# The up-projections of a bilinear MLP by Strassen's seven products over pairs of token blocks

## The chip, the cores and the metric

One core of one Trainium2 chip. The metric is the time of one execution on the device in microseconds (us); lower is better. The profile is one execution of the kernel before; a page and a trace of it are quoted below.

## What is computed

Chunked attention over 64-token chunks gives x (2304 tokens, 512 columns). A first MLP with PReLU and a second, bilinear MLP follow, all in fp32:

```python
def _moe_ref(x, w_in, w_out, alpha):
    h = x @ w_in                                  # 512 -> 2048
    g = np.maximum(h, 0.0) + alpha * np.minimum(h, 0.0)
    return g @ w_out                              # 2048 -> 512

def _moe2_ref(x, w_a, w_b, w_out):
    a = x @ w_a                                   # 512 -> 1536
    b = x @ w_b
    return a * b @ w_out                          # 1536 -> 512
```

The weights arrive as 64-bit floats; the kernel turns them into 32-bit ones itself.

## The kernel before

**Blocks.** The 2304 tokens are five blocks, four of 512 and one of 256 (the second). TensorE (PE) works on float32r operands: every fp32 operand is split into a high part (ScalarE, ACT: `to_hi`, L79) and a low part (VectorE, DVE: `to_lo`, L82), and each product is three matmuls, hi·hi, hi·lo and lo·hi (`three`, L366).

**MLP1.** For each block, J1 = 16 slices j of 128 hidden columns: `s1` (4 x 3 matmuls into a `psh` bank), `prelu` (two ACT, one DVE, then the split into gh, gl), and `s2` (4 x 3 matmuls into four `acc` banks), which runs two slices late (`flush(2)`). In blocks 0 to 3 the attention of the next block is done between these steps. At a block's end `end1` copies the four banks to DRAM (`x2d`), but for the last block, whose result is split directly into the operand of MLP2.

**MLP2.** Blocks outermost (`order2`: the last block first, the short one last), J2 = 12 slices inside. `s3` makes b and a (each 4 x 3 matmuls), multiplies them and splits the product c into ch, cl; `s4` (four token groups, 3 matmuls each, two groups in the short block) adds c times w_out into the `acc` banks, one slice late (`flush(1)`). So PE always has the next `s3` while ACT and DVE make c.

```python
pb = proj(W["b", j], x, n)[:, :n]
...
pa = proj(W["a", j], x, n)[:, :n]
nc.vector.tensor_tensor(out=b_sb, in0=pa, in1=b_sb, op=ALU.mult)
...
split(ch, cl, b_sb)
```

**Weights.** `units` lists 128-column slices in the order of need. `w_load` brings one (512 KB) into one of three staging buffers through SP's queue; `unpack_ops` makes fp32 of it (one ACT at L124, three DVE at L128, L133, L136); `split(*w_parts(i))` makes its two parts. All 36 slices of MLP2 stay in SBUF once split, and are used by all five blocks.

**What orders the work.** The program is written in the order in which each engine runs it (a manual schedule): every engine and SP's DMA queue take their instructions in that order, and one that waits holds all behind it on the same engine. PSUM has eight banks: four in the pool `acc`, four in the pool `ps`. Other pools that matter: `gp` and `tp` (three buffers each), `sp` (three staging buffers), `xp` (two pairs of 512 x 4 operands), `wp` (72 tiles of 128x512).

## Time and profile before

| what | value |
|---|---|
| median of 3 runs | 897.4 us (897.17 to 897.72) |
| the profiled execution: its span, first to last instruction | 895.8 us |
| PE busy, share of the span | 884.1 us, 99% |
| DVE busy | 402.7 us, 45% |
| ACT busy | 352.6 us, 39% |
| mean granted TensorE clock | 0.996 of full |
| DMA: bytes moved | 79.48 MB, mean 89 GB/s |

The profile states a span for its execution and no other time; the median of the runs lies 1.6 us above it. Busy time of PE counts overlapping matmuls once; the pitch of matmuls (from one start to the next) is read from the timeline. A releaser, behind an arrow, is the instruction that ended a wait.

### The profile page before, as it was taken

The page shows a single profiled execution, that of the slowest core. Times are in us where ns is not written, and L with a number is a line of the kernel's source. Part 1 is how long each engine was busy: PE and PEld are TensorE (multiplying, and loading weights), DVE is VectorE, ACT ScalarE, POOL GpSimd, SP SyncE. Part 2 cuts the span into 40 slices and gives each one's busy share as a digit, 9 for nine tenths or more (in the row PEclk, how much of TensorE's full clock was granted, in tenths as well). Part 3 has the DMA queues.
Part 4 walks back from the last instruction along what each step waited for, and adds up shares of the span by engine and source line. Part 5 has one row for each costly group of instructions (what it writes and reads, how often), then busy time and mean ns, then how long its engine had stood idle before and what let it go on. Part 6 is the DMA issues. An engine that isn't in the chain of part 4 may idle for free.

```text
span 895.8 us, 12893 instructions
## 1 busy us (share of the span) xinstructions
PE 884.1 (99%) x5298; PEld 743.9 (83%) x5298; DVE 402.7 (45%) x762; ACT 352.6 (39%) x636; POOL 0.7 (0%) x6
## 2 busy tenths in 40 slices
PE   7999999999999999999999999999999999999998
PEld 6878889988888888888888888888888888888897
DVE  5999955454434443388756742111211122111221
ACT  5687765555436343466534422111211122111211
POOL 0000000000000000000000000000000000000000
PEclk9899999999999999999999999999999999999999
DMA  9686767455425320444414312000020002000100
GB/s 213 199 263 196 213 165 178 107 155 129 106 60 146 79 56 5 141 142 141 148 64 136 124 46 93 2 1 0 1 95 1 0 1 71 1 1 0 48 1 23
DMA packets 127498, 79.48 MB, mean 89 GB/s; under 512 B 94160, under 2 KB 116176, under 8 KB 127440
## 3 DMA queue, kind: packets, MB, share of 16 engines
q1 hardware_dynamic: 127152, 78.41, 31.0%
q8 instruction: 41, 0.67, 0.3%
q10 hardware_dynamic: 288, 0.26, 0.1%
q14 instruction: 17, 0.14, 0.1%
HBM read 53.49 MB, written 16.78 MB: 78 GB/s over the span
## 4 chain that ended last, share of the span: by engine, by line
PE 92%; DVE 6%; ACT 2%; issue 1%; ACTq 0%; POOLq 0%; DVEq 0%; POOL 0%
PE psh L366 52%; PE acc L366 37%; DVE wx L136 1%; PE psSO L291 1%; PE psSO L342 1%; DVE wz L128 1%; DVE wz L133 1%; DVE gl L82 0%; PE psT L278 0%; DVE sm L317 0%; PE warm L625 0%; PE psP L330 0%; DVE e L321 0%; DVE mx L304 0%; DVE e L306 0%
## 5 line engine op out<-in xcount | busy, mean ns | idle before, releaser
L442 DVE TENSOR_TENSOR b_sb<-psh,b_sb 128x512 f32<-128x512 f32 (+1 forms) x60 | 38.3, 638 | 273.2 <-PE psh L366 273.2
L386 DVE SCALAR_TENSOR_TENSOR pos<-neg,nalpha_sb,pos 128x512 f32<-128x512 f32 (+1 forms) x80 | 55.6, 695 | 107.3 <-ACT pos L385 107.0
L440 ACT ACTIVATE b_sb<-psh 128x512 f32<-128x512 f32 (+1 forms) x60 | 33.1, 552 | 168.2 <-PE psh L366 168.2
L79 ACT ACTIVATE ch<-b_sb 128x512 fp32r<-128x512 f32 (+1 forms) x60 | 35.3, 589 | 153.6 <-DVE b_sb L442 153.6
L82 DVE TENSOR_TENSOR gl<-pos,gh 128x512 fp32r<-128x512 f32 (+1 forms) x80 | 51.1, 638 | 43.5 <-ACT gh L79 43.5
L79 ACT ACTIVATE gh<-pos 128x512 fp32r<-128x512 f32 (+1 forms) x80 | 47.2, 590 | 59.0 <-DVE pos L386 59.0
L384 ACT ACTIVATE neg<-psh 128x512 f32<-128x512 f32 (+1 forms) x80 | 43.8, 548 | 40.4 <-PE psh L366 40.4
L82 DVE TENSOR_TENSOR cl<-b_sb,ch 128x512 fp32r<-128x512 f32 (+1 forms) x60 | 38.3, 639 | 39.3 <-ACT ch L79 39.3
L136 DVE SCALAR_TENSOR_TENSOR wx<-wx,wz 128x512 int32<-128x512 int32 x68 | 46.8, 689 | 4.7 <-ACT wx L124 0.8
L124 ACT ACTIVATE wx<-raw 128x512 f32<-128x512 f32 x68 | 42.7, 669 | 4.0 <-DMA raw<-in_moe_w_b_dram 3.8
L385 ACT ACTIVATE pos<-psh 128x512 f32<-128x512 f32 (+1 forms) x80 | 44.2, 553 | 0.0
L128 DVE TENSOR_SCALAR wz<-raw 128x512 uint16<-128x512 uint16 x68 | 29.8, 462 | 3.2 <-DMA raw<-in_moe_w_b_dram 3.2
L133 DVE TENSOR_SCALAR wz<-raw 128x512 uint16<-128x512 uint16 x68 | 31.0, 455 | 0.0
L242 ACT ACTIVATE kqd<-kq 128x1024 uint16<-128x1024 uint16 x24 | 23.9, 1047 | 0.3 <-DMA kq<-in_k_dram 0.3
L79 ACT ACTIVATE xh<-psSO 128x256 fp32r<-128x256 f32 x28 | 8.9, 384 | 25.0 <-PE psSO L342 25.0
L312 ACT ACTIVATE e<-e 128x512 f32<-128x512 f32 x18 | 11.3, 629 | 13.6 <-DVE e L306 13.4
L242 ACT ACTIVATE ed<-e 128x1024 uint16<-128x1024 uint16 x8 | 8.5, 1058 | 17.2 <-DVE e L321 13.6
L321 DVE TENSOR_TENSOR e<-e,rc 128x512 f32<-128x512 f32 x18 | 12.4, 691 | 0.6
L317 DVE TENSOR_REDUCE sm<-e 128x8 f32<-128x512 f32 x18 | 12.2, 680 | 1.0 <-ACT e L312 0.8
L82 DVE TENSOR_TENSOR xl<-psSO,xh 128x256 fp32r<-128x256 f32 x28 | 10.2, 415 | 1.5 <-ACT xh L79 1.5
L304 DVE TENSOR_REDUCE mx<-psSO 128x4 f32<-128x256 f32 x28 | 10.5, 418 | 0.7 <-ACT xh L79 0.7
L291 PEld LDWEIGHTS psSO<-kT,qT 64*64 64x64 f32 x448 | 7.7, 134 | 3.7 <-issue 2.8
(731 smaller groups left out, 2505.7 us busy)
## 6 DMA issues: line engine op xcount, KB each, us to landing
raw<-in_moe_w_out_dram SPq DMA_DIRECT2D x28, 512.0 KB, 3.5
raw<-in_moe_w_in_dram SPq DMA_DIRECT2D x16, 512.0 KB, 4.6
raw<-in_moe_w_b_dram SPq DMA_DIRECT2D x12, 512.0 KB, 4.7
raw<-in_moe_w_a_dram SPq DMA_DIRECT2D x12, 512.0 KB, 3.8
v<-in_v_dram SPq DMA_DIRECT2D x16, 256.0 KB, 4.2
out_dram<-os SPq DMA_DIRECT2D x8, 512.0 KB, 2.8
rowsk<-kqd SPq DMA_DIRECT2D x12, 256.0 KB, 2.1
rowsq<-kqd SPq DMA_DIRECT2D x12, 256.0 KB, 2.5
```

What stands on the lines that cost most here:

```text
L79: nc.scalar.activation(out=hi, in_=src, func=AF.Copy)
L82: nc.vector.tensor_tensor(out=lo, in0=src, in1=hi.bitcast(F32), op=ALU.subtract)
L124: return nc.scalar.activation(out=x.bitcast(F32), in_=hw.bitcast(F32), func=AF.Copy, scale=2.0 ** -112)
L128: yield nc.vector.tensor_scalar(out=z2[:, :, 0], in0=h2[:, :, 1], scalar1=13, scalar2=None, op0=ALU.logical_shift_right)
L133: yield nc.vector.tensor_scalar(out=z2[:, :, 1], in0=h2[:, :, 3], scalar1=1 << 15, scalar2=None, op0=ALU.bitwise_and)
L136: yield nc.vector.scalar_tensor_tensor(out=x, in0=x, scalar=3, in1=z, op0=ALU.logical_shift_left, op1=ALU.bitwise_or)
L366: nc.tensor.matmul(out=ps, lhsT=a, rhs=b, start=(i == 0 and first), stop=(i == n_i - 1 and a is wl))
L384: nc.scalar.activation(out=neg, in_=h, func=AF.Relu, scale=-1.0)
L385: yield nc.scalar.activation(out=pos, in_=h, func=AF.Relu)
L386: yield nc.vector.scalar_tensor_tensor(out=pos, in0=neg, scalar=nalpha_sb[:, j:j + 1], in1=pos, op0=ALU.mult, op1=ALU.add)
L440: nc.scalar.activation(out=b_sb, in_=pb, func=AF.Copy)
L442: nc.vector.tensor_tensor(out=b_sb, in0=pa, in1=b_sb, op=ALU.mult)
```

## The change

MLP2 is put in another order, and its up-projections are computed in another way.

- **Pairs.** The blocks of 512 tokens form two pairs, (0, 2) and (3, 4). With the pair's two blocks as rows, the two halves of the 512 inputs, and w_a, w_b as a 2 x 2 arrangement of halves, seven products of half depth (2 x 3 matmuls each) stand where there were eight. `pair_group(p, j)` issues them into three PSUM banks (A, B, D), three of them added onto a bank that already holds a product, and combines them with seven DVE operations and two ACT copies. The short block keeps its two full products (`rest_group`).
- **Operands.** `sums` and `summed` make four sums of token halves for each pair and split them; for pair 0 the inputs are read from DRAM during the last MLP1 block, for pair 1 two come from DRAM and two straight from the `acc` banks of MLP1's last block (`late_pair`). `weights_steps(j)` unpacks w_a, w_b of slice j, makes four differences (tT) and splits all into T[j] (two buffers).
- **Order.** Slices outermost: for each j the groups of pair 0, the short block (r) and pair 1. Small steps wait in a list `todo2`; `background(us)` takes steps worth so many us out of it at fixed places of a group; `need` takes all up to a mark.
- **c and w_out.** c goes to DRAM unsplit (`keep`); the unpacked w_out is stored to DRAM (`pd`) during the last MLP1 block and read back after pair 0's last group. The last product is a stage of its own at the end: each c is loaded, split, and multiplied, two loads ahead.

```diff
+    full = [b for b in range(NBLK) if sizes[b] == NB]
+    odd = [b for b in range(NBLK) if sizes[b] < NB]
+    pairs = list(zip(full[0::2], full[1::2]))
...
+    order2 = full + odd
+    Q = KD * P // 2
...
-    units += [(m, j) for j in range(J2) for m in "bap"]
+    units += [("p", j) for j in range(J2)] + [(m, j) for j in range(J2) for m in "ab"]
...
-    def s3(j, x, n):
-        pb = proj(W["b", j], x, n)[:, :n]
...
-        nc.scalar.activation(out=b_sb, in_=pb, func=AF.Copy)
...
-        cl = gp.tile([P, NB], F32R, tag="gl", name="cl")[:, :n]
...
-        return ch, cl
+    cd = {(b, j): dr.tile([P, n], F32, name=f"cd{b}_{j}") for b, n in enumerate(sizes) for j in range(J2)}
+    pd = [dr.tile([P, DM], F32, name=f"pd{j}") for j in range(J2)]
+    def keep(b, j, c):
+        nc.sync.dma_start(out=cd[b, j], in_=c)
...
+    def operand(p, q):
+        X[p, q] = [(wtile(f"x{p}{q}h"), wtile(f"x{p}{q}l")) for _ in range(2)]
...
+        for kk in range(2):
+            nc.sync.dma_start(out=X[p, q][kk][1].bitcast(F32), in_=x2d[b][:, 2 * half + kk])
...
+    def sums(p, kk, a21, a22):
...
+        t = {}
+        SUB = ALU.subtract
+        return t, [
+            (0.69, lambda: tt("s1", a21, a22, ALU.add)),
+            (0.69, lambda: tt("s2", lambda: t["s1"], lambda: src("11"), SUB)),
+            (0.69, lambda: tt("s3", lambda: src("11"), a21, SUB)),
+            (0.69, lambda: tt("s4", lambda: src("12"), lambda: t["s2"], SUB)),
+        ]
+    def summed(p, kk, t):
+        def one(q):
+            hl = X[p, q][kk]
+            return [(0.0, lambda: to_hi(*hl, t[q])), (0.69, lambda: to_lo(*hl, t[q]))]
+        return stagger([one(q) for q in ("s1", "s2", "s3", "s4")])
...
+    def stagger(chains):
+        steps = [c[0] for c in chains[:1]]
+        for i, c in enumerate(chains):
+            steps += [d[0] for d in chains[i + 1:i + 2]] + c[1:]
+        return steps
...
+    def weights_steps(j):
...
+        th, tl = xtiles("T")
+        T[j] = th.rearrange("p k n -> p (k n)"), tl.rearrange("p k n -> p (k n)")
+        ua, ub = (units.index((m, j)) for m in "ab")
...
+        def tt(q, a, b):
+            if "t" not in t:
+                t["t"] = sp.tile([P, 2 * DM], F32, tag="stg", name="tT")
+            nc.vector.tensor_tensor(
+                out=t["t"][:, q * Q:(q + 1) * Q], in0=a(), in1=b(), op=ALU.subtract
+            )
...
+        return [
+            (0.0, lambda: (begin(ua), begin(ub))),
+            (0.46, lambda: go(ua)), (0.46, lambda: go(ua)),
+            (0.69, lambda: end(ua, "a")),
+            (0.46, lambda: go(ub)), (0.46, lambda: go(ub)),
+            (0.0, lambda: hi(ca, "a")),
+            (0.69, lambda: end(ub, "b")),
+            (0.0, lambda: hi(cb, "b")),
+            (0.4, lambda: tt(0, part("b", 0), part("a", 0))),
+            (0.4, lambda: tt(1, part("b", 1), part("t", 0))),
+            (0.4, lambda: tt(2, part("b", 1), part("b", 0))),
+            (0.4, lambda: tt(3, part("a", 1), part("t", 1))),
+            (0.0, lambda: hi(ct, "t")),
+            (0.69, lambda: lo(ca, "a")),
+            (0.69, lambda: lo(cb, "b")),
+            (1.2, lambda: lo(ct, "t")),
+        ]
...
+    def product(ps, p, q, j, w, start):
+        th, tl = T[j]
+        for kk in range(2):
+            f = slice(w * Q + kk * P, w * Q + (kk + 1) * P)
+            (wh, wl), (xh, xl) = (th[:, f], tl[:, f]), X[p, q][kk]
+            for i, (a, b) in enumerate(((wh, xh), (wh, xl), (wl, xh))):
+                nc.tensor.matmul(
+                    out=ps, lhsT=a, rhs=b, start=(start and kk == 0 and i == 0),
+                    stop=(kk == 1 and i == 2), skip_group_check=not start,
+                )
...
+    def background(us):
+        while todo2 and us > 0:
+            cost, fn = todo2.pop(0)
+            us -= cost
+            fn()
...
+    def need(key):
+        while key not in ready:
+            todo2.pop(0)[1]()
...
+    def pair_group(p, j, new_bank):
+        A, B, D = (new_bank(nm) for nm in ("psA", "psB", "psD"))
...
+        product(A, p, "11", j, 0, True)
+        p1 = tmp(gp, "gh", "p1")
+        nc.scalar.activation(out=p1, in_=A, func=AF.Copy)
+        product(B, p, "s2", j, 5, True)
+        t1 = tmp(gp, "gl", "t1")
+        tt(t1, p1, B)
+        product(D, p, "s1", j, 4, True)
+        p5 = tmp(tp, "t", "p5")
+        nc.scalar.activation(out=p5, in_=D, func=AF.Copy)
+        product(A, p, "12", j, 1, False)
+        product(B, p, "s3", j, 6, False)
+        background(2.7)
+        t2 = tmp(tp, "t", "t2")
+        tt(t2, p1, B)
+        tt(p5, t2, p5)
+        product(D, p, "s4", j, 3, False)
+        product(B, p, "22", j, 7, False)
+        tt(t1, t1, D)
+        tt(t1, A, t1, ALU.mult)
+        keep(pairs[p][0], j, t1)
+        tt(p1, p1, B)
+        tt(p1, p1, p5, ALU.mult)
+        keep(pairs[p][1], j, p1)
+        background(1.2)
...
+    def rest_group(j):
+        th, tl = T[j]
+        n = sizes[odd[0]]
...
+        pb = half(slice(DM, 2 * DM))
+        b_sb = tp.tile([P, NB], F32, tag="t", name="b_sb")[:, :n]
+        nc.scalar.activation(out=b_sb, in_=pb, func=AF.Copy)
+        pa = half(slice(0, DM))
+        background(2.0)
+        nc.vector.tensor_tensor(out=b_sb, in0=pa, in1=b_sb, op=ALU.mult)
+        keep(odd[0], j, b_sb)
...
+    BG = [0.0, 0.0] + [2.6] * 12 + [6.0, 6.0]
...
+        def go():
+            next(gen[0])
+        def end():
+            next(gen[0])
+            nc.sync.dma_start(out=pd[j], in_=xs.pop(i).bitcast(F32))
+        return [(0.0, begin), (0.46, go), (0.46, go), (0.69, end)]
...
+        done["p"] = 0
+        for j in range(1, 13):
+            early2.setdefault(j, []).append(p_next)
+        early2[1].insert(0, first)
+        for j, fn in (
+            (3, lambda: sums_at(0)), (4, lambda: sums_out(0)), (5, lambda: sums_at(1)), (6, lambda: sums_out(1)),
+            (8, lambda: directs(0, ("11",))), (9, lambda: directs(0, ("12",))), (10, lambda: directs(0, ("22",))),
+            (11, rest_in),
+            (11, lambda: (w_dma(U_AB + 2), todo2.extend(weights_steps(0)))),
+            (13, lambda: (fetch(1, "11", b3, 0), fetch(1, "12", b3, 1))),
+        ):
+            early2[j].append(fn) if j in early2 else early2.update({j: [fn]})
...
+    def late_pair(acc):
...
+        for kk in range(2):
+            def a22(kk=kk):
+                t["a22", kk] = a = wtile("a22", F32)
+                nc.scalar.activation(out=a, in_=acc[2 + kk], func=AF.Copy)
+            t[kk], four = sums(1, kk, lambda kk=kk: acc[kk], lambda kk=kk: t["a22", kk])
+            steps += [(0.0, a22)] + four
+        for kk in range(2):
+            steps += summed(1, kk, t[kk])
+        for kk in range(2):
+            hi, lo = X[1, "22"][kk]
+            steps += [
+                (0.0, lambda hi=hi, lo=lo, kk=kk: to_hi(hi, lo, t["a22", kk])),
+                (0.69, lambda hi=hi, lo=lo, kk=kk: to_lo(hi, lo, t["a22", kk])),
+            ]
+        for q in ("11", "12"):
+            steps += stagger([settled(1, q, kk) for kk in range(2)])
+        todo2.extend(steps)
...
-                if b == NBLK - 1 and j >= 2:
-                    ready = NU1 + 3 * (j - 2) // 2
-                    w_dma(ready + 3)
-                    w_unpack(ready + 1)
-                    w_split(ready)
+                if b == NBLK - 1:
+                    for step in early2.get(j, ()):
+                        step()
+                    background(BG[j] if j < len(BG) else 9.0)
...
+        background(99.0)
+        w_dma(U_AB + 4)
+        mark((0, 0))
+        todo2.extend(weights_steps(1))
+        mark((0, 1))
+        background(3.0)
         flush(0)
...
+        late_pair(acc[0])
+        mark((1, 0))
+        mark((1, 1))
+        seq = [(0, 0), ("r", 0), (0, 1), (1, 0), ("r", 1), (1, 1)]
+        for j in range(2, J2 - 1):
+            seq += [(0, j), ("r", j), (1, j)]
+        seq += [(0, J2 - 1), (1, J2 - 1), ("r", J2 - 1)]
+        left = {j: 3 for j in range(J2)}
+        built = 1
+        for p, j in seq:
+            if j < 2 and p != "r":
+                need((p, j))
+            if p == "r":
+                rest_group(j)
+            else:
+                pair_group(p, j, bank if p == 0 else acc_bank)
+            left[j] -= 1
+            if not left[j] and built + 1 < J2:
+                background(99.0)
+                built += 1
+                w_dma(U_AB + 2 * built + 4)
+                todo2.extend(weights_steps(built))
+            if (p, j) == (0, J2 - 1):
+                for i in range(J2):
+                    W["p", i] = hl = wtile(f"wp{i}h"), wtile(f"wp{i}l")
+                    nc.sync.dma_start(out=hl[1].bitcast(F32), in_=pd[i])
+                todo2.extend(stagger([settle_w(i) for i in range(J2)]))
+        background(99.0)
...
+        order = [(b, j) for b in order2 for j in range(J2)]
+        cs = {}
...
+        def load_c(i):
+            if i < len(order):
+                b, j = order[i]
+                n = sizes[b]
+                hi = gp.tile([P, NB], F32R, tag="gh", name="ch")[:, :n]
+                lo = gp.tile([P, NB], F32R, tag="gl", name="cl")[:, :n]
+                nc.sync.dma_start(out=lo.bitcast(F32), in_=cd[b, j])
+                cs[i] = hi, lo
...
+        for i in range(2):
+            load_c(i)
+        for i, (b, j) in enumerate(order):
+            c = cs.pop(i)
+            split(*c, c[1].bitcast(F32))
+            load_c(i + 2)
...
+            def second(b=b, j=j, c=c):
+                if j == 0:
+                    acc[0] = new_acc()
+                s4(j, c, acc[0], sizes[b])
+                if j == J2 - 1:
+                    end2(b, acc[0])
+            pend.append(second)
+            flush(1)
```

Three places show how the order of the instructions moved. First DVE, where MLP2 begins to need MLP1's last block. Before, after the last `gl` of MLP1 (xl, xh is the operand, wz, wx an unpacking weight, psh a PSUM bank):

```order
L82 TENSOR_TENSOR gl<-pos,gh 128x512
L128 TENSOR_SCALAR wz<-raw 128x512
L133 TENSOR_SCALAR wz<-raw 128x512
L136 SCALAR_TENSOR_TENSOR wx<-wx,wz 128x512
L82 TENSOR_TENSOR wb6l<-wx,wb6h 128x512
L82 TENSOR_TENSOR xl<-acc,xh 128x512 x4
L442 TENSOR_TENSOR b_sb<-psh,b_sb 128x512
```

In the change, between the last operation of group (0, 1) and the first of group (1, 0), DVE has (ss is a sum, x1..h and x1..l the parts of pair 1's operands; three more rows like those of x1s1l to x1s3l, with the sums of the second half, are left out):

```order
L603 TENSOR_TENSOR p_5171<-p_5171,p_5187 128x512
L488 TENSOR_TENSOR ss_5232<-x112l,ss_5207 128x512
L87 TENSOR_TENSOR x1s1l<-ss_5154,x1s1h 128x512
L87 TENSOR_TENSOR x1s2l<-ss_5156,x1s2h 128x512
L87 TENSOR_TENSOR x1s3l<-ss_5158,x1s3h 128x512
L87 TENSOR_TENSOR x1s4l<-ss_5201,x1s4h 128x512
L87 TENSOR_TENSOR x1s4l<-ss_5232,x1s4h 128x512
L87 TENSOR_TENSOR x122l<-a_5152,x122h 128x512
L87 TENSOR_TENSOR x122l<-a_5203,x122h 128x512
L87 TENSOR_TENSOR x111l<-x111l,x111h 128x512 x2
L87 TENSOR_TENSOR x112l<-x112l,x112h 128x512 x2
L603 TENSOR_TENSOR t_5279<-p_5271,psB 128x512
```

Four splits have become one sum and fourteen splits in a row; the product that opens group (1, 0) reads x111.

Second DVE inside a slice. Before, in the first block of MLP2:

```order
L136 SCALAR_TENSOR_TENSOR wx<-wx,wz 128x512
L82 TENSOR_TENSOR wp10l<-wx,wp10h 128x512
L82 TENSOR_TENSOR wb11l<-wx,wb11h 128x512
L442 TENSOR_TENSOR b_sb<-psh,b_sb 128x512
L82 TENSOR_TENSOR cl<-b_sb,ch 128x512
```

In the change, in group (0, 3), two combining operations that read bank B, and between them the unpacking of the next slice's weights:

```order
L603 TENSOR_TENSOR t_5647<-p_5639,psB 128x512
L129 TENSOR_SCALAR wz<-raw 128x512
L134 TENSOR_SCALAR wz<-raw 128x512
L137 SCALAR_TENSOR_TENSOR wx<-wx,wz 128x512
L129 TENSOR_SCALAR wz<-raw 128x512
L134 TENSOR_SCALAR wz<-raw 128x512
L137 SCALAR_TENSOR_TENSOR wx<-wx,wz 128x512
L603 TENSOR_TENSOR t_5682<-p_5639,psB 128x512
```

Before, the unpacking stood behind the product of a slice; now it stands between two reads of a bank that PE writes again.

Third SP's DMA queue towards the end. Before, it held the reload of the next block and the output (xr is a reloaded block, os and ot staged outputs):

```order
L475 DMA xr<-x2d_90 128x1024 x2
L497 DMA out_dram<-os 128x2x512 x2
L475 DMA xr<-x2d_88 128x2x256 x2
L497 DMA out_dram<-os 128x2x512 x2
L491 DMA out_dram<-ot 128x256 x2
```

In the change, from pair 0's last group to the first loads of c (cd is c in DRAM, pd the unpacked w_out there; wp2l to wp10l, which are alike, are left out):

```order
L442 DMA cd_11_98<-t_7069 128x512
L442 DMA cd_11_122<-p_7061 128x512
L1043 DMA wp0l<-pd_147 128x512
L1043 DMA wp1l<-pd_148 128x512
L1043 DMA wp11l<-pd_158 128x512
L442 DMA cd_11_134<-t_7165 128x512
L442 DMA cd_11_146<-p_7157 128x512
L442 DMA cd_11_110<-b_sb 128x256
L1056 DMA cl<-cd_0_87 128x512
L1056 DMA cl<-cd_1_88 128x512
```

The twelve loads of w_out and the last three stores of c stand ahead of the first load of c.

## Rows read from the trace of the kernel before

**Rows 1.** The page: busy time and share by engine; the chain that ended last.
```profile
PE 884.1 (99%) x5298; PEld 743.9 (83%) x5298; DVE 402.7 (45%) x762; ACT 352.6 (39%) x636; POOL 0.7 (0%) x6
PE 92%; DVE 6%; ACT 2%; issue 1%; ACTq 0%; POOLq 0%; DVEq 0%; POOL 0%
```

**Rows 2.** The chain in order of time from 380 us: start, us, what.
```profile
441.00 8.16 PE acc L366 x36
449.16 10.88 PE psh L366 x48
...
829.96 5.44 PE psh L366 x24
...
886.34 2.87 PE psh L366 x24
```

**Rows 3.** Timeline, PE and ACT around 604 us: start, us, engine, instruction.
```profile
603.81 0.39 PE L366 MATMUL psh<-yh,wb7l 128*128 128x512 f32 x1
604.04 0.39 PE L366 MATMUL psh<-yh,wa7h 128*128 128x512 f32 x1
...
604.30 0.60 ACT L440 ACTIVATE b_sb<-psh 128x512 f32<-128x512 f32 x1 [4.07 <-PE psh L366]
```

**Rows 4.** DVE by form: busy us, mean ns of one | idle before.
```profile
L136 DVE SCALAR_TENSOR_TENSOR wx<-wx,wz 128x512 int32<-128x512 int32 x68 | 46.8, 689 | 4.7 <-ACT wx L124 0.8
L442 DVE TENSOR_TENSOR b_sb<-psh,b_sb 128x512 f32<-128x512 f32 x48 | 33.2, 692 | 238.1 <-PE psh L366 238.1
L133 DVE TENSOR_SCALAR wz<-raw 128x512 uint16<-128x512 uint16 x68 | 31.0, 455 | 0.0
L306 DVE TENSOR_TENSOR e<-psSO,mx 128x256 f32<-128x256 f32 x28 | 10.4, 415 | 0.0
L82 DVE TENSOR_TENSOR yl<-xr,yh 128x1024 fp32r<-128x1024 f32 x6 | 7.3, 1225 | 1.5 <-ACT yh L79 1.5
```

**Rows 5.** Timeline of DVE in MLP1's last block.
```profile
430.38 0.69 DVE L136 SCALAR_TENSOR_TENSOR wx<-wx,wz 128x512 int32<-128x512 int32 x1
430.99 0.68 DVE L82 TENSOR_TENSOR wa4l<-wx,wa4h 128x512 fp32r<-128x512 f32 x1
431.59 0.69 DVE L82 TENSOR_TENSOR wp4l<-wx,wp4h 128x512 fp32r<-128x512 f32 x1
...
438.23 0.69 DVE L82 TENSOR_TENSOR gl<-pos,gh 128x512 fp32r<-128x512 f32 x1 [0.70 <-ACT gh L79]
```

**Rows 6.** ACT by form: busy us, mean ns of one | idle before.
```profile
L124 ACT ACTIVATE wx<-raw 128x512 f32<-128x512 f32 x68 | 42.7, 669 | 4.0 <-DMA raw<-in_moe_w_b_dram 3.8
L79 ACT ACTIVATE ch<-b_sb 128x512 fp32r<-128x512 f32 x48 | 30.3, 632 | 135.2 <-DVE b_sb L442 135.2
```

**Rows 7.** DMA issues: count, KB each, median us from issue to landing.
```profile
raw<-in_moe_w_b_dram SPq DMA_DIRECT2D x12, 512.0 KB, 4.7
raw<-in_moe_w_a_dram SPq DMA_DIRECT2D x12, 512.0 KB, 3.8
out_dram<-os SPq DMA_DIRECT2D x8, 512.0 KB, 2.8
rowsk<-kqd SPq DMA_DIRECT2D x12, 256.0 KB, 2.1
...
xr<-x2d SPq DMA_DIRECT2D x2, 256.0 KB, 4.5
...
out_dram<-ot SPq DMA_DIRECT2D x2, 128.0 KB, 1.8
```

**Rows 8.** Windows of 2 us: busy PE, PEld, DVE, ACT, POOL; granted clock, DMA share, GB/s.
```profile
18.00:20.00 2.00, 0.56 (x4) 0.42 (x4) 1.90 (x6) 1.11 (x2) 0.00 (x0) 1.00 1.11 223
20.00:22.00 2.00, 1.31 (x36) 1.20 (x36) 1.58 (x5) 1.89 (x6) 0.00 (x0) 0.71 0.20 6
22.00:24.00 2.00, 1.73 (x39) 1.21 (x41) 1.61 (x5) 1.58 (x3) 0.00 (x0) 0.50 0.26 70
24.00:26.00 2.00, 2.00 (x44) 1.88 (x37) 2.00 (x7) 1.66 (x5) 0.00 (x0) 0.50 0.48 193
26.00:28.00 2.00, 2.00 (x13) 2.00 (x12) 2.00 (x7) 1.24 (x3) 0.00 (x0) 0.58 0.31 54
...
36.00:38.00 2.00, 1.61 (x7) 1.01 (x6) 2.00 (x4) 1.08 (x2) 0.00 (x0) 1.00 0.80 270
```

More of the change, by code (lines that the diff above doesn't have):

```diff
@@ L472, in reload @@
-    def reload(b):
-        for e in range(0, KD, 2):
-            s = sp.tile([P, 2, DM], F32, tag="stg", name="xr")[:, :, :sizes[b]]
-            nc.sync.dma_start(out=s, in_=x2d[b][:, e:e + 2])
-            yield s
-    def resplit(e, s, x2):
-        n = s.shape[2]
-        split(x2[0][:, e:e + 2, :n], x2[1][:, e:e + 2, :n], s)
+            s = sp.tile([P, 2, DM], F32, tag="stg", name="xs")[:, :, :n]
+            copy2(s, acc, e, n)
+            nc.sync.dma_start(out=x2d[b][:, e:e + 2], in_=s)
@@ new lines, in sums, with src, tt @@
+    def sums(p, kk, a21, a22):
+        def src(q):
+            return X[p, q][kk][1].bitcast(F32)
+        def tt(nm, a, b, op):
+            t[nm] = wtile(f"s{nm}", F32)
+            nc.vector.tensor_tensor(out=t[nm], in0=a(), in1=b(), op=op)
+        t = {}
[6 more added lines that the diff above has]
+        ]
@@ new lines, in late_pair @@
+    def late_pair(acc):
+        for q in ("22", "s1", "s2", "s3", "s4"):
+            operand(1, q)
+        t = {}
+        steps = []
+        for kk in range(2):
[14 more added lines that the diff above has]
+            steps += stagger([settled(1, q, kk) for kk in range(2)])
+        todo2.extend(steps)
```

161 lines of the change are left out of this document (113 added, 48 removed).

## The prediction

> **What bounds the kernel now.** I read the page's busy times first: PE is busy for 99% of the span and makes 92% of the chain that ended last, while DVE and ACT stand at 45% and 39% [rows 1]. Then the chain in order of time: from 441 us to the end it is matmuls without a gap, 36 in 8.16 us, then 48 in 10.88 us, to the short block's 24 in 2.87 us [rows 2]. So a matmul of 512 columns costs 8.16/36 = 0.2267 us from start to start, one of 256 columns 2.87/24 = 0.1196 us, and MLP2 begins at 449.16 us with nothing to gain but matmuls: whatever is taken away counts in full, and every new wait of PE counts in full. The timeline gives the price of a hand-over: wb7l's last matmul is followed by the next 0.23 us later, and ACT's copy of the bank starts 0.26 us after that [rows 3]; I use 0.27 us. DVE to ACT and back cost 0.03 to 0.1 us.
>
> **What is taken away.** A pair and slice had 2 x 24 matmuls and has 7 x 6 = 42. Two pairs, 12 slices: 144 matmuls x 0.2267 = **32.6 us less**. The short block and the last product keep their matmuls. A product of six takes 1.36 us, a pair group 9.52 us, the short block's group 2.87 us.
>
> **What is added, and its cover.** Per slice DVE has 14 combining operations at 0.692, two unpackings (2 x (0.455 + 0.455 + 0.689)), four differences at 0.415, splits of 0.692, 0.692 and 1.225 and a short product of about 0.42: 17.6 us [rows 4] under 2 x 9.52 + 2.87 = 21.9 us of PE. So DVE is not the bound on average, and the cost is in places where PE must wait. Back to back, DVE starts independent operations of this size every 0.605 us [rows 5], dependent ones every 0.72 us.
>
> *End of MLP1.* Unpacking w_out, the sums and the splits of pair 0 lie under PE, about 5.0 us of DVE in each 5.44 us slice. Behind the gl of slice 14, whose equivalent ends at 438.9 us [rows 5], stand b's unpacking, the differences and splits of T[0]: 6.3 us with the pitches above, then slice 15's own 2.1 us. Its gl ends at 447.2 us, and the second matmul of its s2 wants it at 441.0 + 24 x 0.2267 + 0.23 = 446.7 us: **0.6 us** (0 to 4, should the loads of pair 0, five of 512 KB and six of 256 KB at once with the stores, hold DVE up).
>
> *Slice 1's weights.* SP sends them only behind the store of the last unpacked w_out, about 1 us before PE starts group (0, 0); w_b is issued 0.5 us later and takes 4.7 us [rows 7], so it lands 4.2 us after that start. ACT has its widening (0.67) and a split (0.63) [rows 6] ahead of the copy p1 (0.60 [rows 3]), which frees bank A only 6.1 us after the start, and the fourth product wants it at 4.08 us: **2.0 us** (0 to 2.5).
>
> *Pair 1's operands.* DVE ends group (0, 1) 1.7 us after PE does (0.27, then two operations). Then come the last sum and ten splits up to the one that PE's second matmul of (1, 0) reads, x111's first: 12 starts at 0.605 = 7.3 us. PE stands from 0.23 to 9.0 us: **8.8 us** (8 to 11; at 0.69 each it is 9.8). Nothing covers it; in the before kernel s3 did, with the operand's four splits under MLP1's last matmuls.
>
> *Slice 2's weights.* They are issued behind the stores of (1, 0), about 2.2 us after it, land 3.8 and 4.7 us after issue [rows 7], and again stand ahead of p1, now of group (1, 1): 1.7 us. T[2] is then finished in a row: its low part of w_a comes 1.9 us after PE wants it, and 0.4 us go at the bank turns. **4.0 us** (2.5 to 6). From slice 3 on loads are a slice ahead.
>
> *Inside pair 0's groups.* Weights of the next slice stand between t1 and t2. t1 starts at 2.72 + 0.27 = 3.0 us; ACT widens w_a only behind p5 (4.35 + 0.6 + 0.65 = 5.6); then wx, two half steps and wx on DVE bring t2 to 7.75 us and its end to 8.45 us, and the product that writes its bank wants to start at 8.16 us: **0.3 us x 9 slices = 2.7 us** (0 to 6).
>
> *w_out and c through DRAM.* SP's order after group (0, 11) is twelve loads, three stores, then c. With 2.7 us for 256 KB (I take it between the 2.1 us of a 256 KB write and the 3.8 us of a 512 KB read) and 0.7 us for each that follows (512 less 256 KB of writes, 2.8 - 2.1) [rows 7], w_out's fourth lands 7.1 us on; its split stands ahead of t2: 0.9 us. After (1, 11) DVE has five splits (3.0 us) ahead of the short product, whose store goes out at 15.9 us; c is issued at 16.4, lands at 19.1 and is split by ACT at 19.7 us. PE ended at 9.52 + 0.9 + 2.87 = 13.3 us. **7.5 us** in all (6 to 11).
>
> *The last stage.* A load may start when the product three before it has ended: 0.3 + 2.7 + 0.05 + 0.63 + 0.05 + 2.72 = 6.5 us against 3 x 2.72 = 8.16 us: hidden, with up to 4.3 us for a load. For the short block, 0.3 + 2.3 + 0.5 + 1.37 = 4.5 us against 4.1 us, three or four times: **1.7 us** (0.5 to 5; 2.3 us lies near the 1.8 us of a 128 KB write).
>
> *The clock.* The granted clock fell to 0.71 and 0.50, half of full and so 1.2 of 2.4 GHz, after 2 us in which PE was busy for 0.56 us, and stayed there while PE was dense again, to within 26 to 28 us [rows 8]. From 24 to 28 us that lost 2 x 0.5 + 2 x 0.42 = 1.8 us, with 20 to 24 us 3.4 us. The two long waits (8.8 and 6.6 us) should each bring this; I take 2.1 us, near the dense part alone: **4.2 us** (0 to 7). The Trainium skill ("TensorE: Matmul & The Clock Gate", Part 1) says that an idle array goes to half clock and must be busy for a while to get it back; this trace agrees.
>
> **The sum.** Waits: 0.6 + 2.0 + 8.8 + 4.0 + 2.7 + 7.5 + 1.7 + 4.2 = 31.5 us. Against 32.6 us that leaves 1.1 us: a span of 894.7 for 895.8, and 897.4 - 1.1 = **896.3 us** for the median, which lies 1.6 us above the span. The forecast is that Strassen's saving is nearly given back, above all in two waits at the borders of the new stages. A measurement here can tell some 0.2%, 1.8 us, from no change.
>
> **Rivals.**
> *Cover is better.* DVE's 45% leaves room, and if the clock stays up or comes back at once, t2 is in time and slice 1's weights arrive early, 4.2 + 2.7 + 2.0 us fall away: 887.4 us. For it: a wait of 0.39 us in the window from 36 to 38 us left the clock at full [rows 8]. Against: the waits of 8.8 and 6.6 us are much longer. 20%.
> *Late in the middle of pair 0's groups: slower.* PE writes bank B again at 8.16 us, my chain ends at 8.45 us, and each 0.1 us more costs 0.9 us. Five hand-overs between ACT and DVE stand in it; at 0.15 us more each the wait is 1.0 us and the time 896.3 + 9 x 0.7 = 902.6 us. It decides from a wait of 0.7 us (899.9 and more). 15%.
> *Loads of c bound the last stage: slower.* If 256 KB take the 4.5 us of the reload behind two output stores [rows 7], the loop is 8.3 to 8.8 us against 8.16: up to 0.6 x 16 = 9.6 us, and the short block 6 us more: 911.9 us. Against: one load at a time, on an idle queue. 5%.
> *The clock swings in every group: slower.* The short waits of nine slices would each cost a spell of half clock, 9 x 2.1 = 19 us: 915.2 us. Rows speak against it (full clock across a 0.39 us wait [rows 8]). The Trainium skill, on the same page ("A second HAM failure mode"), tells of a kernel that cycles through PSUM banks, idles briefly between groups and swings between the two clocks; by that rule this change would be worse off, and no row here shows it. 5%.
> *The change doesn't remove the matmuls.* PE's program is shorter by exactly 144, so I give this nothing.
>
> **How the numbers follow.** The forecast has 55%; its own range is 891 to 901 us from the bounds above, taken as independent. Below 895.6 us it is faster (22 of the 55), within 1.8 us same (20), above 899.2 slower (13). With the rivals: faster 0.22 + 0.20 = 0.42, same 0.20, slower 0.13 + 0.25 = 0.38. The range 887 to 907 us takes in the forecast, better cover and the late middle, and leaves out the last two rivals and tails, under 0.2.
>
> **What would show it.** 144 matmuls fewer; PE idle for about 9 us before x111's product and 6 to 7 us before the first product of the last stage, each followed by a granted clock near 0.5; a wait near 0.3 us before the seventh product of pair 0's groups; none in the last stage's full blocks. I am wrong if PE's waits outside the two borders exceed 15 us, or if either border is covered.

## The result, and the profile after

| kernel | median | range, runs |
|---|---|---|
| before | 897.5 us | 897.17 to 897.72, 4 |
| changed | 902.63 us | 901.62 to 904.39, 4 |

The ratio is 1.0058, 95% interval 1.0044 to 1.0073: slower by 0.6%, 6.3 us above the forecast and inside its range. A run's time is 1.8 us more than its span, before and after. The profiled execution has 899.8 us; its span is 5.1 us above the forecast one.

The page of the changed kernel, to be held against [rows 1] (the PEclk line is the granted clock in 40 slices, in tenths):

```profile
span 899.8 us, 13238 instructions
PE 864.0 (96%) x5154; PEld 717.5 (80%) x5154; DVE 525.9 (58%) x976; ACT 373.5 (42%) x668; POOL 0.7 (0%) x6
PEclk9999999999999999999997999999999999999999
```

144 matmuls are gone, as said, and PE is busy for 20 us less. What it now waits for is in the waits of PE from 440 us on (total, times, longest); the same view of the kernel before is empty in this stretch:

```profile
PE acc L367 <- ACT ch L84: 7.8, 2, 6.0
PE psA L573 <- ACT x111h L84: 4.6, 1, 4.6
PE psA L573 <- ACT p L607: 3.8, 2, 2.3
PE psA L573 <- DVE x111l L87: 3.6, 1, 3.6
PE psA L573 <- DVE Tl L87: 1.7, 1, 1.7
PE psB L573 <- DVE t L603: 1.4, 1, 1.4
PE acc L367 <- DVE gl L87: 0.2, 1, 0.2
```

Where they stand, and what comes behind them, is in PE's timeline (start, duration, engine, instruction, wait before it):

```profile
449.88 0.39 PE L573 MATMUL psA<-x011h,Th 128*128 128x512 f32 x1
...
455.69 0.50 PE L573 MATMUL psA<-x012h,Th 128*128 128x512 f32 x1 [1.57 <-ACT p L607]
...
478.43 0.80 PE L573 MATMUL psA<-x111h,Th 128*128 128x512 f32 x1 [4.56 <-ACT x111h L84]
482.83 0.79 PE L573 MATMUL psA<-x111l,Th 128*128 128x512 f32 x1 [3.60 <-DVE x111l L87]
...
503.41 0.66 PE L573 MATMUL psA<-x112h,Th 128*128 128x512 f32 x1 [2.28 <-ACT p L607]
...
742.78 0.80 PE L367 MATMUL acc<-wp0h,ch 128*128 128x512 f32 x1 [5.99 <-ACT ch L84]
...
881.65 0.50 PE L367 MATMUL acc<-wp3h,ch 128*128 128x512 f32 x1 [1.84 <-ACT ch L84]
...
885.00 0.63 PE L367 MATMUL acc<-wp4h,ch 128*128 128x512 f32 x1
```

Matmuls that take 0.63 us and more are at half clock. First the window that holds the wait at slice 1, 1.57 us, then one at or behind each long wait (columns as in [rows 8]; the granted clock is the figure behind POOL):

```profile
452.00:456.00 4.00, 2.43 (x11) 1.73 (x10) 3.24 (x7) 2.72 (x5) 0.00 (x0) 1.00 0.36 128
480.00:484.00 4.00, 1.17 (x3) 0.98 (x4) 4.00 (x8) 0.00 (x0) 0.00 (x0) 0.50 0.00 0
504.00:508.00 4.00, 4.00 (x13) 3.14 (x12) 2.66 (x7) 2.05 (x3) 0.00 (x0) 0.62 0.35 119
742.00:746.00 4.00, 3.22 (x8) 2.51 (x9) 2.08 (x3) 1.89 (x3) 0.00 (x0) 0.51 0.24 93
882.00:886.00 4.00, 4.00 (x12) 3.07 (x11) 0.86 (x3) 0.42 (x1) 0.00 (x0) 0.57 0.10 33
```

Four spells at half clock, where the forecast had two; the wait of 1.57 us at 455 us brought none.

**The account.** "Lost" is counted so: from each product's first matmul to the next product's I take the difference of the starts, less the product's matmuls at 0.2267 us (0.1196 with 256 columns). What is left over is lost. (The 0.29 us of pair 0's groups are such a loss, spread over the starts of two matmuls; the view of PE's waits has none of them.) The kernel before loses 0.2 us in its whole MLP2, the changed one 36.3 us, and 0.7 more ahead of it:

| term of the forecast | forecast | measured | of it at half clock |
|---|---|---|---|
| End of MLP1 | 0.6 | 0.7 | |
| Slice 1's weights | 2.0 | 1.9 | |
| Pair 1's operands | 8.8 | 10.8 | 1.9 |
| Slice 2's weights | 4.0 | 6.6 | 1.8 |
| Inside pair 0's groups (nine) | 2.7 | 2.6 | |
| w_out and c through DRAM | 7.5 | 9.4 | 1.6 |
| The last stage | 1.7 | 4.7 | 1.7 |
| The clock (in the rows above) | 4.2 | | 7.0 |
| sum | 31.5 | 36.7 | 7.0 |

The parts come to within 0.3 us of 37.0. Against 32.6 us saved that is 4.4 us, and the span is 4.0 us longer.

The last wait's cause, in the chain in order of time (start, duration, what): the load of c stands on SP behind both output stores of the block before, and takes 4.03 us beside them.

```profile
875.64 0.02 ACT os L456
875.66 0.47 issue
876.13 0.42 ACT ch L84
876.55 0.41 SPq L662
...
877.04 4.03 DMA cl<-cd
...
881.18 0.42 ACT ch L84
```

### The profile page after: what moved, and what is told of

Its sections match the earlier page's. It is cut to its first block, busy times and chain, and to the rows that moved or that the text cites. A ratio compares the mean times of both kernels' runs of the same rounds, so it can differ in the third digit from the quotient of the medians.

```text
span 899.8 us, 13238 instructions
## 1 busy us (share of the span) xinstructions
PE 864.0 (96%) x5154; PEld 717.5 (80%) x5154; DVE 525.9 (58%) x976; ACT 373.5 (42%) x668; POOL 0.7 (0%) x6
## 5 line engine op out<-in xcount | busy, mean ns | idle before, releaser
L87 DVE TENSOR_TENSOR cl<-cl,ch 128x512 fp32r<-128x512 f32 (+1 forms) x60 | 38.3, 639 | 109.1 <-ACT ch L84 103.8
L84 ACT ACTIVATE ch<-cl 128x512 fp32r<-128x512 f32 (+1 forms) x60 | 35.3, 589 | 109.4 <-DMA cl<-cd 73.2
L603 DVE TENSOR_TENSOR t<-p,psB 128x512 f32<-128x512 f32 x48 | 32.8, 684 | 56.7 <-PE psB L573 55.1
L607 ACT ACTIVATE p<-psA 128x512 f32<-128x512 f32 x24 | 14.3, 596 | 76.0 <-PE psA L573 75.3
L613 ACT ACTIVATE p<-psD 128x512 f32<-128x512 f32 x24 | 14.3, 597 | 47.7 <-PE psD L573 45.6
L367 PE MATMUL psr<-xrh,Tl 128*128 128x256 f32 x96 | 27.2, 283 | 0.0
L367 PE MATMUL psr<-xrl,Th 128*128 128x256 f32 x96 | 27.2, 283 | 0.0
L367 PE MATMUL psr<-xrh,Th 128*128 128x256 f32 x96 | 27.1, 283 | 0.0
L84 ACT ACTIVATE Th<-wx 128x512 fp32r<-128x512 f32 x24 | 15.1, 630 | 12.2 <-DVE wx L137 12.2
L84 ACT ACTIVATE Th<-tT 128x1024 fp32r<-128x1024 f32 x12 | 12.7, 1062 | 14.8 <-DVE tT L535 14.8
```

Source lines behind the costliest of these rows:

```text
L84: nc.scalar.activation(out=hi, in_=src, func=AF.Copy)
L87: nc.vector.tensor_tensor(out=lo, in0=src, in1=hi.bitcast(F32), op=ALU.subtract)
L367: nc.tensor.matmul(out=ps, lhsT=a, rhs=b, start=(i == 0 and first), stop=(i == n_i - 1 and a is wl))
L603: nc.vector.tensor_tensor(out=out, in0=a, in1=b, op=op)
```

## The experiments

The theory: the waits above are separate, each has the cause that the forecast named, and a long one costs a spell at half clock besides. The rivals: DVE's amount of work is the bound, so that a wait taken away at one place comes back at the next; or the spells cost nothing, since what follows a wait is paced by the engine that PE waited for. Every run has the kernel before beside it (897.5 to 897.6 us); "lost" is the account above from the start of MLP2, in the profiled execution.

| run | median, us | ratio to before (95%) | lost, us |
|---|---|---|---|
| changed kernel | 902.63 | 1.0058 (1.0044 to 1.0073) | 36.3 |
| 1 slice 2's loads early | 899.04 | 1.0017 (1.0006 to 1.0027) | 32.8 |
| 2 c five products ahead | 898.87 | 1.0015 (1.0004 to 1.0026) | 34.7 |
| 3 the border | 896.67 | 0.9987 (0.9975 to 0.9998) | 29.2 |
| 4 idle matmuls in the waits | 894.83 | 0.9973 (0.9964 to 0.9982) | 15.1 + 17.0 |
| 5 splits in the order of need | 898.62 | 1.0012 (1.0002 to 1.0021) | 31.9 |
| 6 t2 first | 921.35 | 1.0265 (1.0244 to 1.0285) | 55.4 |
| 7 all of it together | 899.17 | 1.0020 (1.0010 to 1.0029) | 34.4 |
| 8 and the short group first | 896.77 | 0.9988 (0.9979 to 0.9998) | 31.9 |
| 9 one step less ahead of t2 | 900.77 | 1.0032 (1.0020 to 1.0043) | 33.4 |
| 10 "all_b" | 878.05 | 0.9789 (0.9776 to 0.9802) | 12.6 |
| 11 "all_c" | 877.67 | 0.9778 (0.9765 to 0.9791) | 13.3 |
| 12 all_c and two more | 877.78 | 0.9789 (0.9776 to 0.9802) | 10.7 |

### 1. Slice 2's loads early

```diff
                 need((p, j))
+            if (p, j) == (0, 1):
+                w_dma(U_AB + 6)
```

> Edit: SP issues the loads of slice 2's w_a and w_b ahead of group (0, 1), some 32 us sooner than behind the stores of (1, 0). Nothing else moves. Theory (the loads are late): around groups (1, 1) and (0, 2) the changed kernel loses 6.9 us against dense matmuls: 2.3 us of wait before x112's product, 1.7 us before the first matmul that reads the low part of T[2], the rest at half clock or in short gaps. Loads that have long landed take away 5 to 6.9 us of it: median 895.7 to 897.6 us for 902.6. Rival (DVE is the bound there): the 17 steps of T[2] need T[0]'s tiles, which come free only behind (1, 0), and about 8 us of DVE beside 5 us of combining have 12.4 us of PE to hide under; then the wait before x112's product goes but comes back at the first matmul that reads T[2]'s low part; the gain is under 2.5 us, median above 900 us.

Measured 3.6 us less: between the two theories, under the 5 us of the first and above the 2.5 of the rival. The longer of the two waits behind p1 is gone and with it a spell; the wait for T[2]'s low part stays (waits of PE):

```profile
PE psA L573 <- DVE Tl L87: 1.7, 1, 1.7
PE psA L573 <- ACT p L607: 1.6, 1, 1.6
```

Of 6.6 us 2.3 are left. So 4.3 us belonged to the loads, and 2.3 us to T[2]'s own chain on DVE, where the rival is right.

### 2. c five products ahead

```diff
-                hi = gp.tile([P, NB], F32R, tag="gh", name="ch")[:, :n]
-                lo = gp.tile([P, NB], F32R, tag="gl", name="cl")[:, :n]
+                hi = wtile("ch")[:, :n]
+                lo = wtile("cl")[:, :n]
...
-            load_c(i + 2)
+            load_c(i + 5)
```

> Edit: the tiles of c in the last stage come from the pool of 72 weight tiles, and a load is issued five products ahead instead of two. The instructions of PE, ACT and DVE are the same; on SP two or three more loads stand ahead of the output stores of each block. Theory (loads queue behind the output stores): the last stage loses 0.5 us at the third product of the second block and 4.2 us in the short block (2.1 us of wait, 1.7 us at half clock, 0.4 us in short gaps); all of it goes: median about 898.0 us (897.6 to 898.8) for 902.6, no wait and full clock from 746 us to the end. Rival (a load of c is simply too slow for the short block's products of 1.37 us, or the banks' copies on ACT hold the split up): a deeper queue moves the wait by a product or two, the gain is under 1.5 us, median above 901 us.

Behind its first product the last stage has no wait and loses nothing: all 4.7 us are gone, and the theory holds. The median fell by 3.8 us only, just past the slow end of the theory's range. In the profiled execution, the slowest of nine (900.75 us, the fastest 895.95), another term had grown: slice 2's loads, which this edit doesn't touch, cost 8.8 us, not 6.6. ACT's second widening starts at 502.21 us in the changed kernel and here at 503.98:

```profile
503.98 0.67 ACT L125 ACTIVATE wx<-raw 128x512 f32<-128x512 f32 x1 [1.66 <-DMA raw<-in_moe_w_b_dram]
```

The load of w_b, issued at 497.30 us, needed 6.7 us; in the changed kernel, issued at 497.69, it took 4.5. In both, three loads of 512 KB were under way at once. A load of c behind the output stores still takes 3.7 us here; it is only asked for sooner.

### 3. The border

```diff
             if (p, j) == (0, J2 - 1):
+                for i in range(2):
+                    load_c(i)
...
-                todo2.extend(stagger([settle_w(i) for i in range(J2)]))
+                todo2.extend(stagger([settle_w(i) for i in range(2)]))
```

The other ten w_out splits stand in the last stage's loop, two products ahead of their use.

> Edit: the first two loads of c are issued ahead of the twelve loads of the unpacked w_out, behind group (0, 11); and only two of the twelve w_out splits stand ahead of the last stage, the others are made two products ahead inside it. Theory (the border waits for a load that is queued behind the short product's store, and t2 of (1, 11) for a split whose w_out tile lands late): of the 9.4 us that are lost there, 1.5 at t2, 6.2 of wait and 1.6 at half clock, only the way from the short product's end over DVE to the first split of c is left, 0.3 + 0.4 + 0.7 + 0.2 = 1.6 us, and the clock stays up: gain 6.5 to 8 us, median 894.5 to 896 us. Rival (DVE and ACT have a backlog at the border whatever is loaded): the first product starts no sooner than about 741 us and the splits that are moved into the last stage hold its products up; gain under 3 us, median above 899.5 us.

Measured 6.0 us less, under the theory's 6.5 to 8; of the border's 9.4 us 2.9 are left. The load, the wait of 6 us and the spell went. The 1.5 us at t2 of (1, 11) stayed, because two w_out splits still stand ahead of it on DVE and their tiles land no sooner. The short block showed something else: PE waited 1.9 us at the same place, and the clock did not fall (windows of this run; PE busy for 2.10 of 4 us in the first):

```profile
872.00:876.00 4.00, 2.10 (x9) 1.27 (x8) 0.78 (x3) 0.81 (x3) 0.00 (x0) 1.00 0.79 268
876.00:880.00 4.00, 4.00 (x19) 3.02 (x17) 0.93 (x4) 0.83 (x2) 0.00 (x0) 1.00 0.18 48
```

### 4. Idle matmuls in the waits

```diff
+    def busy(n, w):
+        ps = bank("idle")
+        for _ in range(n):
+            nc.tensor.matmul(out=ps, lhsT=w[:, :P], rhs=X[0, "11"][0][0], start=True, stop=True)
...
+                if (p, j) == (1, 0):
+                    busy(36, T[1][0])
```

and likewise 8, 24 and 7 in the other three waits.

> Edit: in the four long waits PE runs matmuls that nobody reads, into a bank that is free: 36 before (1, 0), 8 before x112's product of (1, 1), 24 before the last stage, 7 before the fourth product of the short block (0.2267 us each, a little less than each wait). Nothing else changes, and no wait is removed. Theory (each long wait also costs a spell at half clock): the four spells lost 1.9, 1.8, 1.6 and 1.7 us; they go, 7.0 us in all, the waits for x111 and ch end at the same times as before: median 895.6 us (895 to 897.5), granted clock 1.00 through. Rival (what follows each wait is paced by the engine that PE waited for, so slow matmuls there cost nothing): the spells go, but their time is then waited for; gain under 2 us, median above 900.6 us.

Measured 7.8 us less, and faster than the kernel before, by 75 matmuls that nobody reads. x111l's product starts 32.8 us after the start of MLP2, for 33.0 without them. The clock holds in all four places (windows of this run):

```profile
484.00:488.00 4.00, 4.00 (x19) 3.33 (x18) 0.70 (x2) 0.94 (x2) 0.00 (x0) 1.00 0.00 0
502.00:506.00 4.00, 4.00 (x20) 3.30 (x19) 3.83 (x8) 1.60 (x2) 0.00 (x0) 1.00 0.04 13
740.00:744.00 4.00, 4.00 (x19) 3.34 (x18) 2.08 (x3) 1.90 (x3) 0.00 (x0) 1.00 0.34 125
880.00:884.00 4.00, 4.00 (x19) 3.04 (x18) 0.47 (x2) 0.61 (x2) 0.00 (x0) 1.00 0.22 66
```

So the spells are a cost of their own and not hidden by what follows: in the four places this execution loses 23.1 us, the idle matmuls counted as lost, and the changed kernel 29.6. The 6.4 us between them are most of the 7.0 of the account. The Trainium skill ("TensorE: Matmul & The Clock Gate", Part 1) tells of the gate that halves an idle array's clock; the trace agrees (0.50 to 0.62 behind these waits in the changed kernel, 1.00 here).

Elsewhere something got worse. PE's wait for t2 of (1, 11), 1.4 us in the changed kernel, is 3.0 us in this execution, the slowest of ten (896.99 us): the w_out tiles landed later, and a spell came with it (waits, window). It loses 4.5 us there, for 1.7.

```profile
PE psB L573 <- DVE t L603: 3.0, 1, 3.0
728.00:732.00 4.00, 2.74 (x7) 2.17 (x8) 3.18 (x5) 1.75 (x3) 0.00 (x0) 0.57 0.68 255
```

### 5. Splits in the order of need

```diff
-        for kk in range(2):
-            steps += summed(1, kk, t[kk])
...
-        for q in ("11", "12"):
-            steps += stagger([settled(1, q, kk) for kk in range(2)])
+        for qs in (("11", "s2", "s1"), ("12", "s3"), ("s4", "22")):
+            todo2.extend(stagger([split_of(q, kk) for q in qs for kk in range(2)]))
+            mark(qs)
```

> Edit: the same 22 steps that make pair 1's operands (eight sums, fourteen splits), the splits in the order in which the products of (1, 0) read them: x111, s2 and s1 ahead of the group, x112 and s3 behind its t1, s4 and x122 behind t2; in the changed kernel x111 and x112 came last. Theory (the order, not the amount, costs the 10.8 us): PE waits for DVE's end of group (0, 1), 1.7 us, for the last sum and one split, 3.0 us in all, then a product of 1.36 us covers the two splits of 1.21 us of the next one; with a spell at half clock of up to 1.9 us some 5 us are left: gain 5 to 8 us, median 894.5 to 897.5 us. Rival (DVE's amount of work decides, 22 operations of 0.6 us): the wait is only spread over the products of (1, 0), gain under 2.5 us, median above 900 us.

Measured 4.0 us less, below the theory's 5 to 8 and above the rival's 2.5. The loss in (1, 0) falls from 10.8 to 7.7 us. The wait at the first product is now 2.7 us, not 8.2, but it brings its spell all the same, and new waits stand behind it (waits of PE): x112's high part is queued on ACT behind p5, which needs the product before.

```profile
PE psA L573 <- DVE x111l L87: 2.7, 1, 2.7
PE psB L573 <- DVE t L603: 2.0, 2, 1.3
PE psA L573 <- ACT x112h L84: 1.2, 1, 1.2
```

### 6. t2 first

```diff
-        background(2.7)
         t2 = tmp(tp, "t", "t2")
         tt(t2, p1, B)
         tt(p5, t2, p5)
+        background(2.7)
```

> Edit: in every pair group the steps for the next weights stand on DVE behind t2 and its follower, not ahead of t2. Theory (t2's end is late for the seventh product, as forecast): the 0.29 us in each of nine slices of pair 0 and part of the 1.5 us at t2 of (1, 11) go: 2.6 to 4 us, median 898.6 to 900 us; T[j] still has 22 us for 17.6 us of DVE work and is in time. Rival (nothing is gained, since the seventh product waits on the bank for another reason, or the next slice's weights get late in turn): median 902 us or above.

The theory is wrong: 18.7 us more. The rival's "902 us or above" came true, but the weights that got late are the smaller part of it. The nine waits of 0.29 us went, and nine of 1.0 to 1.4 us came, 1.3 us lost in each slice. The 3.2 us of weights steps now stand ahead of the operation that frees bank D, and with that a bank for the short block's second half (DVE's timeline, then PE's):

```profile
575.83 0.69 DVE L603 TENSOR_TENSOR p<-t,p 128x512 f32<-128x512 f32 x1
576.44 0.46 DVE L129 TENSOR_SCALAR wz<-raw 128x512 uint16<-128x512 uint16 x1
...
579.47 0.68 DVE L603 TENSOR_TENSOR t<-t,psD 128x512 f32<-128x512 f32 x1
```

```profile
580.20 0.39 PE L367 MATMUL psr<-xrh,Th 128*128 128x256 f32 x1 [1.04 <-DVE t L603]
```

Pair 0 and the short block share four banks, and a slice needs five. So the place of these steps is bounded on both sides, t2 on the one and the bank on the other. Pair 1's operands, T[2] and the border lost 9 us more together.

### 7 and 8. All of it together; the short block's group first

Runs 1, 2, 3, 5 and 6 in one kernel, with slice 1's loads issued ahead of the last pd store. In the second,

```diff
-        seq = [(0, 0), ("r", 0), (0, 1), (1, 0), ("r", 1), (1, 1)]
+        seq = [(0, 0), ("r", 0), (0, 1), ("r", 1), (1, 0), (1, 1)]
```

> Edit: all of it together: slice 2's loads early, c five products ahead, the border's loads and splits, the need order, t2 first, and the loads of slice 1's weights ahead of the store of the last unpacked w_out. Theory (the terms are separate and add): of 37.2 us lost against dense matmuls there are left 0.7 at the end of MLP1, up to 1 for slice 1, 5 for pair 1, 2.3 at T[2], 2 to 3 at the border: some 12 us; span about 875 us, median 876 to 880 us, 2% under the kernel before. Rival (what one wait gives back the next takes, since DVE is the bound from 440 to 520 us): the loss there stays near 15 us, median 884 us or above.

> Edit: as in the run with all of it together, and the short block's group of slice 1 is put ahead of (1, 0), so that its 2.87 us of matmuls lie under DVE's splits for pair 1. Theory (any matmuls that need nothing late are cover): the 3 us of wait before (1, 0) and the clock spell behind it go; T[2], which has only (1, 1) left to be made under, is up to 2.9 us later and may cost that at the first matmul that reads its low part: 2 to 5 us less than all of it together. Rival (DVE is the bound there): the wait moves to T[2] in full, the same time within 1 us.

The first missed by 19 us, for two reasons. It carries run 6's edit, whose waits for the bank are the largest of all and lose 11.8 us. And the rival was right too: (1, 0) and T[2] lose 19.3 us, where the theory left 7.3 and the rival some 15 (waits of PE):

```profile
PE psr L367 <- DVE t L603: 9.4, 9, 1.0
PE psA L573 <- DVE x111l L87: 5.0, 1, 5.0
PE psA L573 <- DVE Tl L87: 4.3, 1, 4.3
```

Slice 1's 1.9 us went. The waits for the bank are also nine regular ones of 1.0 us, and the granted clock stays at full across them (windows of this run):

```profile
524.00:528.00 4.00, 2.96 (x25) 2.76 (x24) 3.83 (x8) 1.54 (x3) 0.00 (x0) 1.00 0.42 131
528.00:532.00 4.00, 4.00 (x20) 3.32 (x20) 3.97 (x8) 1.55 (x2) 0.00 (x0) 1.00 0.34 131
```

The second is 2.4 us faster than the first, within what the theory said: the wait for x111l falls from 5.0 to 1.3 us, while the one for T[2]'s low part grows from 4.3 to 4.8.

### 9. One step less ahead of t2

```diff
-        background(2.7)
+        background(2.5)
```

> Edit: against the changed kernel only the amount of weights steps between t1 and t2 of every pair group: one DVE operation of 0.69 us less stands ahead of t2 (2.53 us of steps, not 3.2), and one more behind the group. When all of the steps stood behind t2, the short block's second half waited 1.3 us a slice for the bank that t1's next operation frees. Theory (t2 was 0.3 us late, and the bank has some 2 us of slack that 0.69 us do not use up): the nine waits of 0.29 us go and nothing takes their place, 2.6 us less, about 900 us. Rival (the slack is smaller, or the next weights get late): no gain, 902 us or above.

The nine waits of 0.29 us are gone from the trace and none takes their place. The median is 1.9 us lower, for 2.6 expected; its runs spread from 896.93 to 902.94 us, so the size is left open, not the mechanism.

### 10 to 12. The kernel that beats both

All_b is run 8 with the steps ahead of t2 again, and the splits of x112, s3 and s4 ahead of p5. All_c adds run 9's edit. The last adds

```diff
-            if (p, j) == (0, J2 - 1):
+            if (p, j) == (1, J2 - 2):
                 for i in range(2):
                     load_c(i)
...
             (0.0, lambda: hi(cb, "b")),
+            (0.69, lambda: lo(ca, "a")),
```

> Edit: as the run with the short block's group first, but the weights steps stand ahead of t2 again, as in the changed kernel, and ACT's and DVE's splits for x112, s3 and s4 stand right behind t1 of (1, 0), ahead of p5. Theory (the waits of that run were the bank of the short block's second half, 13.6 us in ten slices, and a split that was queued behind p5): those go; left are 0.7 at the end of MLP1, 2.6 inside pair 0's groups, some 2 for pair 1, 2 to 4 at T[2], 2 to 3 at the border: 10 to 12 us for 37.2, span 873 to 876, median 875 to 878 us. Rival (DVE is the bound from 460 to 520 us, so T[2] takes up what pair 1 gives back): 4 to 6 us more, 880 to 884 us.

> Edit: as the run before this one (all_b), with one DVE operation of weights steps less ahead of t2. Theory (the waits add): 2 to 2.6 us less than all_b. Rival (with the other waits gone, DVE's backlog makes the weights late): the same or more.

> Edit: as the run all_c, and two more: the loads of w_out and of the first two tiles of c are issued one group sooner, behind (1, 10) and not behind (0, 11), and the first low part of each T[j] is split as soon as its w_a is unpacked, ahead of the four differences. Theory (two waits are left, t2 of (1, 11) behind a late w_out split, 4.2 us with its short gaps, and T[2]'s low part behind the differences, 5.8 us with its spell): the first goes but for 0.3 us, the second shrinks by 1.4 to 3 us, because the first product of (0, 2) then runs under the rest: span about 870 us, median 870.5 to 873 us. Rival (the loads meet the weights' steps, or the low part only makes the differences late by as much): 876 us or above.

All_b came as the theory had it: 12.6 us lost, 878.05 us. With the weights steps ahead of t2 again and the splits ahead of p5, (1, 0), (1, 1) and T[2] lose 6.8 us, so the amount of DVE's work was not what kept run 7 back there. The separate waits add up once none is in another's way: runs 1, 2, 3 and 5 alone gave 17.3 us together, all_b, with slice 1's loads and the short block's group moved as well, gives 24.6. What PE still waits for there from 440 us on, waits under 0.3 us left out, with 4.9 us lost at T[2] (the waits):

```profile
PE psA L573 <- DVE Tl L87: 3.3, 1, 3.3
PE psB L573 <- DVE t L603: 2.1, 2, 1.4
PE acc L367 <- DVE cl L87: 0.7, 1, 0.7
```

All_c gave nothing that can be told from it: the 2.6 us inside the groups went, but in its profiled execution the border cost 5.5 us for 2.7 (t2 of (1, 11) behind a later w_out load, with a spell), and T[2] 5.8 for 4.9, as its rival had it. The last run missed; its rival was right. The w_out split now holds up t2 of (0, 11), one group sooner, as its tile lands only at 705.9 us (ACT's timeline), and at T[2] the high part of the differences is late in place of the low part of w_a; 6.0 us are lost there.

```profile
705.90 0.63 ACT L84 ACTIVATE wp0h<-wp0l 128x512 fp32r<-128x512 f32 x1 [2.13 <-DMA wp0l<-pd]
```

## Why the forecast was wrong, step by step

In sum 36.7 us were lost, for 31.5 in the forecast. Of the 5.2 us between them the clock has 2.8, more than half; the last stage has 1.3, slice 2's weights and t2 of (1, 11) 0.8 each, and the wait for c at the border gives 0.4 back; the other terms are right to 0.1. So the change, forecast at 1.1 us faster, came out 5.1 us slower.

**Right.** The 32.6 us, each matmul's pitch, and the place of every wait but one, the 0.5 us in the last stage's full blocks. Slice 1's weights (1.9 for 2.0), the operands of pair 1 without the clock (8.9 for 8.8), the nine waits of 0.29 us and the wait for c at the border (6.2 for 6.6) came within half a microsecond, from rows of the kernel before alone. At (1, 0) the sum was right and its parts were not: PE stood 4.6 us ahead of the first matmul already, for ACT's x111h, which the forecast left out, and 3.6 us ahead of the second. DVE's x111l set the end of both, so the total is the forecast's. "Strassen's saving is nearly given back" is what happened; it was a little more than given back.

**Wrong, the clock: 7.0 us for 4.2.** The step "the two long waits should each bring this" failed. Waits of 2.3 and 1.84 us brought a spell too, so there were four. The size of one was right (1.6 to 1.9 us for 2.1). The forecast had rows for a wait of 0.39 us and for 2 us with 0.56 us busy [rows 8], and took the waits between for the harmless kind without saying so. Yet those 2 us hold a single wait, of 1.71 us, among small matmuls of the attention: no longer than the waits that the forecast passed over (kernel before, PE's timeline):

```profile
19.45 0.63 PE L330 MATMUL psP<-ident,e 128*128 128x128 f32 x4 [1.71 <-ACT eT L332]
```

Run 4 shows that this cost is separate.

**Wrong, the last stage: 3.0 us for 1.7 without the clock.** "2.3 us lies near the 1.8 us of a 128 KB write" chose the wrong row. The load behind two output stores took 4.03 us, and [rows 7] had its like, the 4.5 us of the reload behind two output stores; the text used that only for a rival in which every load is so slow. The full blocks were not wholly hidden either, 0.5 us, again behind stores. Run 2 takes both waits away.

**Wrong, slice 2's weights: 4.8 us for 4.0 without the clock.** Run 1 parts it: 2.3 us are T[2]'s own chain, as forecast (1.9 and 0.4), the rest is the loads. Those were issued when the forecast said, 2.1 us behind (1, 0), but the issue of w_a alone held SP for 1.55 us, for 0.39 at slice 1 (SP's timeline):

```profile
496.04 1.55 SPq L108 DMA_DIRECT2D raw<-in_moe_w_a_dram  x1
497.69 0.46 SPq L108 DMA_DIRECT2D raw<-in_moe_w_b_dram  x1
```

So w_b landed 8.2 us behind (1, 0), for 6.9 in the forecast, though it took 4.5 us from its issue, for 4.7. ACT made its split behind p1 and not ahead of it, which gave 0.6 us back. What held SP is open; a third load was under way, but run 1, with two at this place, has an issue of 1.36 us as well.

**Wrong, t2 of (1, 11): 1.7 for 0.9,** a w_out tile that landed later: the fourth 7.7 us behind group (0, 11), for 7.1.

**Wrong, the step from span to median.** The median of the changed kernel lies 2.8 us above the profiled span, and not 1.6: that execution was the fastest of four, and its like spread over 2.8 us where the kernel before spreads over 0.6. Run 2's 8.8 us for 6.6 at slice 2 shows one place where unchanged code varies: waits that end with loads move with the loads.

**The rivals.** "Late in the middle of pair 0's groups" gave 902.6 us, near the result, but is refuted: its wait was 0.29 us. "The clock swings in every group" is refuted as well: across nine waits of 0.29 us, and of 1.0 us in run 7, the clock stayed at full. The Trainium skill ("TensorE: Matmul & The Clock Gate", "A second HAM failure mode") tells of a kernel that swings so between groups; no run here shows it at these lengths. "Loads of c bound the last stage" was right in kind for the first loads behind a block's stores alone, and "better cover" was not there but could be made: all_b and all_c are at 878 us.
